# A linear-attention kernel's first step: two levels of products formed over both half chunks at once

## The chip, the cores and the metric

The kernel runs on one core of a Trainium2 chip. The metric is the device time of one execution in microseconds, as the median of several. A core has TensorE (PE in the profile, with its weight loads as PEld), VectorE (DVE), ScalarE (ACT), GpSimd (POOL) and SyncE (SP, which issues most DMAs). Each takes the instructions of its own queue in order; semaphores tie the queues together.

## The reference

Two blocks follow one another, all in fp32. The first is a linear attention with a state that decays (4 batches, 8 heads, 768 tokens, 48 channels a head); the second a feed-forward block (384 to 2048 to 384) with an activation, on the 3072 rows that the first one gives.

```python
def _attn_ref(r, k, v, w, u):
    B, H, S, D = r.shape
    state = np.zeros((B, H, D, D), dtype=np.float32)
    y = np.zeros_like(r)
    for t in range(S):
        kt, vt, rt, wt = (k[:, :, t], v[:, :, t], r[:, :, t], w[:, :, t])
        cur = np.einsum('bhd,bhe->bhde', u[None] * kt, vt)
        y[:, :, t] = np.einsum('bhd,bhde->bhe', rt, state + cur)
        state = wt[:, :, :, None] * state + np.einsum('bhd,bhe->bhde', kt, vt)
    return y.astype(np.float32)

def _moe_ref(x, w_in, w_out):
    h = x @ w_in
    sp = np.maximum(h, 0.0) + np.log1p(np.exp(-np.abs(h)))
    g = h * erf(sp)
    return (g @ w_out).astype(np.float32)
```

## The kernel before

The tokens are cut into chunks of 128, and each chunk into two half chunks of 64 (`HC`). A step handles one chunk of two batches; twelve steps follow one another. Within a step the attention of a half chunk on itself is built by levels, 1 to 6 (`LOG`): at level n the tokens stand in blocks of 2^n, and the right half of each block (`rights`) meets the left half. A level has three parts. `level_products` (L669 to 685) forms k by r on TensorE, for every pair of heads (`n`, 8 of them), every half chunk (`s0`) and the two heads of the pair (`e`), which lie on partitions 0 to 47 and 64 to 111: 8 x 2 x 2 = 32 products a level. Each product has the keys as its weights (its columns are key tokens) and 32 query tokens as its moving side. Result and half chunk share partitions: the first half chunk fills PSUM partitions 0 to 63, the second 64 to 127. `scale` (L357 for one of two batches of head pairs, L364 for all) multiplies k and r in place by decay totals, for the next level. `take_level` or `take_blocks` then copies what counts out of PSUM into `own`, which holds key tokens on partitions and query tokens along the row.

The first step is written apart, in `attend_first`. There the products of a level come in two batches of four head pairs (`halves`), each followed by its scaling, so that VectorE scales one batch while TensorE forms the other. Two PSUM tiles (`banks`) take turns. Between two levels `keep_busy` (L1008) issues a 128 x 128 by 384 matmul with zeros into the tile whose turn is next; it must wait until the level before has been copied out of it. Levels 2 to 4 are copied by VectorE with a mask (`take_level`, L691), level 5 (`MASKED`) by ScalarE in four copies of 16 partitions (`take_blocks`, L712), level 6 by ScalarE in two copies of 32 partitions (`take_level`, L698). At level 5 a product has 48 weight columns (64 less the 16 that meet nothing), at level 6 it has 32.

Behind level 6 the step goes on: eight transposes of k (L957), `from_own` (L725: `own` times v, one part before and one after the new state), `state_part` (L800), `through_state` (L751), a hop of some channels by matmul (L766), and then the second step, whose level 1 products (L681) stand around that hop. The second step takes in the first pieces of the feed-forward block: `hidden` (L1171) multiplies by w_in, 12 records at a time, between the levels. Meanwhile the weights come in and are converted: DMAs issued by SyncE, a scaling by ScalarE (L289, L297), a shift by VectorE (L306), an addition by GpSimd (L319). The order on each queue is the order in which the program's calls stand.

Of the kernel before, what the change touches and what calls it, by code (L numbers as in the profile page):

```python
# [21 lines left out]
HC = 64  # L22
# [21 lines left out]
LOG = 6  # L44
MASKED = 5
# [7 lines left out]
def rights(ap, half):  # L53

    names = "abcdefg"[: len(ap.shape) - 1]
    spread = " ".join(names)
    return ap.rearrange(f"{spread} (n two h) -> {spread} n two h", two=2, h=half)[
        (slice(None),) * len(names) + (slice(None), 1)
    ]
# [32 lines left out]
def kernel(  # L92
# [14 lines left out]
    nc = tc.nc  # L107
    PSUM = bass.MemoryType.PSUM

    n_steps, _, _, JP, C = rkw.shape  # L110
    NH, D = v.shape[2:]
    NP = JP // NJ
    NE = NH // JP
# [50 lines left out]
    def products(shape, n=None):  # L164

        if n is None:
            n = turns["next"]
            turns["next"] = 1 - n
        names = "abc"[: len(shape) - 1]
        return banks[n][:].rearrange(  # L170
            f"p ({' '.join(names)}) -> p {' '.join(names)}", **dict(zip(names, shape[1:]))
        )
# [164 lines left out]
    def rows(e, n=D):  # L337
        return slice(e * EP, e * EP + n)
# [314 lines left out]
    def parts_of(s):  # L653

        c, i = divmod(s, SPC)
        in_t, vt = loaded[s]
        made, tots, tot = ready[s]
        ends = tot.rearrange("p (n h) -> p n h", h=NC)
        return c, in_t, vt, made, states[i][c % 2], states[i][1 - c % 2], ends

    def by_pair(t):

        return lambda x, n: t[:, x, n]

    def first_pair(x, n):

        return turns["first"][:, n // NP, x, n % NP]

    def level_products(pp, rk, level, ns=range(NJ * NP)):  # L669

        half = 1 << (level - 1)
        m = HC - half if 1 < level <= MASKED else HC if level == 1 else half
        for n in ns:
            for s0 in range(0, C, HC):
                for e in range(NE):
                    right = rk(0, n)[rows(e), s0 : s0 + HC]
                    to = pp[s0 : s0 + m, e, n, :]
                    if level > 1:
                        right = rights(right, half)
                        to = to[:, : HC // 2].rearrange("p (b h) -> p b h", h=half)  # L680
                    nc.tensor.matmul(  # L681
                        to, lhsT=rk(1, n)[rows(e), s0 : s0 + m], rhs=right,
                        start=True,
                        stop=True,
                    )

    def take_level(own, pp, level):
        half = 1 << (level - 1)
        got = pp[:].rearrange("p e n t -> p (e n) t")
        if level <= MASKED:  # L690
            nc.vector.copy_predicated(  # L691
                rights(own[:], half),
                rights(mask_sb[:, level - 1 : level, :].to_broadcast([P, NH, HC]), half),
                got[..., : HC // 2].rearrange("p n (b h) -> p n b h", h=half),
            )
        else:
            for s0 in range(0, C, HC):
                nc.scalar.copy(own[s0 : s0 + half, :, half:], got[s0 : s0 + half, :, :half])  # L698
# [2 lines left out]

    def take_blocks(own, pp, level):

        half = 1 << (level - 1)
        got = pp[:].rearrange("p e n t -> p (e n) t")
        for s0 in range(0, C, HC):
            for b in range(HC // 2 // half):
                of = slice(s0 + 2 * b * half, s0 + (2 * b + 1) * half)  # L710
                t = (2 * b + 1) * half
                nc.scalar.copy(  # L712
                    own[of, :, t : t + half], got[of, :, b * half : (b + 1) * half]
                )

    def from_own(s, own, swap):
        vt = loaded[s][1]
# [170 lines left out]
    def attend_first(xT):  # L888


        for _ in prepare(0):
            pass
        totals = plan_totals(0)
        c, _, vt, made, S, S_next, ends = parts_of(0)
        t5 = turns["first"]
        own = att.tile([P, NH, HC], FP32, name="own")
        halves = [range(j * NP, (j + 1) * NP) for j in range(NJ)]
        batch = JP * C // 2 // NJ
        pp = products([P, NE, JP, HC])
        for half in halves:  # L900
            level_products(pp, by_pair(made), 1, half)
            stay_warm(2)
        nc.scalar.copy(first[:], mask_sb[:, 0, :])
        totals(1, part=slice(0, batch))
        for j in range(NJ):
            scale(0, 1, batch=j)
        load_second(t5[:, 1, 0, NP - 1, 1:2])

        def wait_for(t):

            nc.gpsimd.tensor_copy(out=block_sb[:, 0:1], in_=t5[:, 1, 0, NP - 1, t : t + 1])

        wait_for(1)
        totals(1, part=slice(batch, 2 * batch))
        totals(2, part=slice(0, batch // 2))
        nc.vector.tensor_mul(
            own[:], pp[:].rearrange("p e n t -> p (e n) t"),
            first[:, None, :].to_broadcast([P, NH, HC]),
        )
        behind = {3: (3,), 4: (4, 5), 5: (6,)}  # L920
        for level in range(2, LOG):
            pp = turns.pop("pp", None) or products([P, NE, JP, HC])
            for j, half in enumerate(halves):
                level_products(pp, first_pair, level, half)
                scale(0, level, batch=j)
            turns["pp"] = products([P, NE, JP, HC])
            keep_busy(turns["pp"], (DM,))
            (take_blocks if level == MASKED else take_level)(own, pp, level)
            wait_for(1 << level - 1)
            if level == 2:  # L930
                totals(2, part=slice(batch // 2, batch))
            else:
                totals(*behind[level])
            if level == 2:
                stages["b"](0, 0)
                stages["b"](0, 1)
                stages["r"](0)
                second = prepare(1)
                next(second)
                nc.sync.dma_start(out=vt[:], in_=v[0])  # L940
                stages["l"](1, own[:, 0, 2:3])
                nc.sync.dma_start(out=ws[1][:], in_=rkw[1][:, 2])
        totals = plan_totals(1)
        pp = turns.pop("pp")
        for j, half in enumerate(halves):
            level_products(pp, first_pair, LOG, half)
            scale(0, LOG, batch=j)
        take_level(own, pp, LOG)
        wait_for(HC - 1)
        next(second)  # L950

        kT = att.tile([P, NH, D], FP32, name="kT", bufs=1)
        kT_by_e = kT[:].rearrange("p (e n) d -> p e n d", e=NE)
        turned = products([P, JP, P])
        turns["next"] = 1 - turns["next"]
        for n in range(JP):
            nc.tensor.transpose(turned[:, n, :], first_pair(1, n), ident[:])  # L957
        from_own(0, own, 1)
        for half, copy in zip(halves, (nc.vector.tensor_copy, nc.scalar.copy)):
            copy(  # L960
                kT_by_e[:, :, half.start : half.stop],
                turned[:, half.start : half.stop].rearrange("p n (e d) -> p e n d", e=NE)[..., :D],
            )
        stages["h"](0)
        fence()
        stages["l"](2, seen[:, 0:1])
        load_v(1)
        stages["h"](0)
        ps = [[products([P, NE, JP, HC], 1 - e)[:, e] for e in range(NE)]]
        state_part(0, kT, ps, (0,))  # L970
        from_own(0, own, 0)
        nc.scalar.copy(middle[rows(1)], ps[0][1][rows(1), :, :D])
        nc.vector.tensor_copy(middle[rows(0)], ps[0][0][rows(0), :, :D])
        stages["o"](0)
        nc.gpsimd.tensor_mul(faded[1][:], middle[:], ends[:, :, 1:2].to_broadcast([P, JP, D]))
        through_state(0, xT)
        stages["b"](1, 0)
        stages["b"](1, 1)
        stages["r"](1)
        stages["h"](1)  # L980
        stages["h"](1)
        totals(1)
        stages["o"](1)
        totals(*range(2, LOG + 1))

        def pending():
            part = products([P, NE, JP, HC], turns["next"])[:, 0]
            state_part(0, kT, ps + [[part] * NE], (1,))
            nc.vector.tensor_add(S_next[both], faded[1][both], part[both, :, :D])
            load_third()  # L990
            stages["l"](5, S_next[:, 0, 0:1])

        turns["pending"] = pending
# [560 lines left out]
    for kk in range(KT):  # L1554
        n = D // KT
        to, of = (x.rearrange("p (e m) -> p e m", e=NE) for x in (apart[:, kk], ident[:]))
# [189 lines left out]
```

## Time and profile before

| what | value |
|---|---|
| median of three runs | 573.74 us |
| the three runs | 572.72, 574.93, 573.74 us |
| the profiled execution, its own time | 573.87 us |
| its span in the profile | 572.1 us |
| PE busy | 563.2 us (98% of the span) |
| DVE, ACT, POOL busy | 453.9, 358.2, 248.5 us |
| products of levels, L681: matmul records | 2368 in the program, 33.9 us busy |
| w_in products, L1171 | 960 records, 214.9 us busy |
| first step | about 0 to 26 us |
| granted TensorE clock in the first 30 us and after | 1.00 |

The page gives each engine's busy time and its share of the span; PE is a matmul's time from its start to a modelled end, and matmuls overlap, so that 98% does not mean that the array is full. An fp32 matmul appears as two records of MATMUL and two of LDWEIGHTS, so 32 products are 64 records of each. In a row `48*48 48x32` stands for weights of 48 rows by 48 columns and 32 tokens that move. "issue" as the cause of idle time means that the engine waited for nothing that the profile shows.

### The profile page before, as it was taken

How to read it: one execution, taken by the hardware profiler on the slowest of the kernel's cores; microseconds unless marked ns; L12 is line 12 of the kernel's file. 1: busy time of each engine (PE TensorE's matmuls, PEld its weight loads, DVE VectorE, ACT ScalarE, POOL GpSimd, SP SyncE). 2: the span in 40 equal slices, each digit the busy share in tenths (PEclk: the TensorE clock that was granted, in tenths of full speed). 3: DMA queues.
4: the chain of work that ended last, by engine and by line, in shares of the span. 5: the costliest groups of instructions: out<-in, count | busy, mean ns of one | idle time of the engine just before them, and what ended most of it. 6: DMA issues, size and time to landing. Idle time of an engine off the chain costs nothing.

```text
span 572.1 us, 16721 instructions
## 1 busy us (share of the span) xinstructions
PE 563.2 (98%) x7318; PEld 500.4 (87%) x7318; DVE 453.9 (79%) x505; ACT 358.2 (63%) x494; POOL 248.5 (43%) x268
## 2 busy tenths in 40 slices
PE   8899999999999999999999999999999999999997
PEld 5688887678998998998998998898898899989997
DVE  8684886999899998799699599599599596477730
ACT  3658877745458858747756766766675771489500
POOL 4757390732885883384285185176075000000000
PEclk9999999999999999999999999999999999999999
DMA  7596672440425315245245235235332201000000
GB/s 267 190 311 255 226 222 59 171 162 7 148 86 167 107 60 167 37 157 169 33 140 180 40 126 195 40 112 167 47 112 84 47 9 34 3 2 1 28 29 28
DMA packets 54081, 63.24 MB, mean 111 GB/s; under 512 B 35160, under 2 KB 40568, under 8 KB 52984
## 3 DMA queue, kind: packets, MB, share of 16 engines
q1 hardware_dynamic: 53480, 61.98, 34.5%
q8 instruction: 57, 0.93, 0.7%
q10 hardware_dynamic: 528, 0.20, 0.1%
q14 instruction: 16, 0.13, 0.1%
HBM read 52.39 MB, written 8.69 MB: 107 GB/s over the span
## 4 chain that ended last, share of the span: by engine, by line
PE 92%; DVE 4%; ACT 1%; issue 1%; DMA 1%; DVEq 0%; ACTq 0%
PE m L1171 35%; PE m L1293 33%; PE c L1396 6%; PE pp L681 6%; PE m L1203 4%; PE y L725 2%; PE y L751 2%; PE pp L800 2%; DVE in L364 1%; DMA in<-in_rkw 1%; PE pp L1081 1%; PE pp L1008 1%; DVE h L1136 1%; PE c L1293 0%; PE m L999 0%
## 5 line engine op out<-in xcount | busy, mean ns | idle before, releaser
L1171 PE MATMUL m<-xT,w_in_sb 128*128 128x256 f32 x960 | 214.9, 382 | 0.3 <-ACT h L1180 0.3
L1171 PEld LDWEIGHTS m<-xT,w_in_sb 128*128 128x128 f32 x960 | 179.9, 190 | 25.5 <-ACT h L1180 0.8
L364 DVE TENSOR_TENSOR in<-in,tot_sb 128x1024 f32<-128x1024 f32 (+1 forms) x55 | 77.8, 1415 | 6.5 <-PE pp L681 4.4
L1180 ACT COPY h<-m 128x512 f32<-128x512 f32 x80 | 46.2, 579 | 48.6 <-PE m L1171 48.4
L1293 PE MATMUL m<-mixed,h 128*128 128x192 f32 x320 | 56.7, 331 | 0.0
L1293 PE MATMUL m<-w_out_sb,h 128*128 128x192 f32 x320 | 56.1, 329 | 0.0
L1293 PEld LDWEIGHTS m<-mixed,h 128*128 128x128 f32 x320 | 51.8, 190 | 0.9
L1293 PEld LDWEIGHTS m<-w_out_sb,h 128*128 128x128 f32 x320 | 52.0, 190 | 0.5
L1293 PE MATMUL m<-w_out_sb,room 128*128 128x192 f32 x288 | 49.7, 326 | 0.0
L1293 PEld LDWEIGHTS m<-w_out_sb,room 128*128 128x128 f32 x288 | 47.3, 190 | 0.1
L1131 ACT ACT_TABLE_LOAD x28 | 35.9, 1283 | 10.7 <-DVE h L1136 8.5
L503 POOL TENSOR_TENSOR words<-words,own 128x384 f32<-128x384 f32 x21 | 30.1, 1434 | 22.8 <-DVE words L534 13.0
L544 POOL TENSOR_TENSOR words<-words 128x384 f32<-128x384 f32 x28 | 39.7, 1448 | 0.0
L681 PEld LDWEIGHTS pp<-in 48*48 48x48 f32 (+4 forms) x2368 | 30.1, 120 | 10.5 <-issue 5.8
L1127 ACT ACT_TABLE_LOAD x28 | 35.9, 1283 | 1.8 <-issue 1.3
L496 POOL TENSOR_TENSOR own<-rest 128x384 f32<-128x384 f32 x7 | 9.7, 1382 | 61.0 <-ACT o L1299 61.0
L681 PE MATMUL pp<-in 48*48 48x32 f32 (+4 forms) x2368 | 33.9, 206 | 0.0
L544 POOL TENSOR_TENSOR rk<-words 128x384 f32<-128x384 f32 x28 | 33.4, 1224 | 0.0
L569 DVE TENSOR_REDUCE sums<-rk 128x16 f32<-128x768 f32 (+2 forms) x31 | 31.6, 1020 | 0.0
L448 POOL TENSOR_TENSOR tot_sb<-tot_sb 128x256 f32<-128x256 f32 (+4 forms) x50 | 28.9, 578 | 3.8
L1127 ACT ACTIVATE room<-h 128x1024 f32<-128x1024 f32 x28 | 29.6, 1057 | 0.3
L319 POOL TENSOR_TENSOR w_out_sb<-w_out_sb,rest 128x768 int32<-128x768 int32 x8 | 18.3, 2292 | 21.6 <-DVE w_out_sb L311 21.6
(217 smaller groups left out, 1010.7 us busy)
## 6 DMA issues: line engine op xcount, KB each, us to landing
in<-in_rkw SPq DMA_DIRECT2D x8, 1024.0 KB, 5.5
words<-in_moe_w_in SPq DMA_DIRECT2D x16, 384.0 KB, 5.3
words<-in_moe_w_out SPq DMA_DIRECT2D x16, 384.0 KB, 5.8
words<-in_rk_rows SPq DMA_DIRECT2D x8, 768.0 KB, 5.9
w<-in_rkw SPq DMA_DIRECT2D x11, 512.0 KB, 7.4
v<-in_v SPq DMA_DIRECT2D x12, 384.0 KB, 5.6
out<-o SPq DMA_DIRECT2D x23, 192.0 KB, 3.0
in<-in_rkw SPq DMA_DIRECT2D x7, 512.0 KB, 5.8
```

Source lines behind the costliest of these rows:

```text
L364: nc.vector.tensor_mul(halves, halves, view(tots[level - 1], 0, [[1, n], [2, nb], [0, half]]))
L448: nc.gpsimd.tensor_mul(new, pair[:, :, 0], pair[:, :, 1])
L503: engine.tensor_mul(to, to, of[:, :, None, :].to_broadcast([P, NEAR // 2 // half, half, D]))
L544: engine.tensor_mul(to[:, i], r[:, half:], k[:, part * rows + i, None].to_broadcast([P, half, D]),)
L569: nc.vector.tensor_reduce(out=to, in_=of, axis=mybir.AxisListType.X, op=ALU.add)
L681: nc.tensor.matmul(to, lhsT=rk(1, n)[rows(e), s0 : s0 + m], rhs=right, start=True, stop=True,)
L1127: nc.scalar.activation(sp_room, chunks[0], AF.Softplus)
L1131: nc.scalar.activation(at, sp_room, AF.Erf)
L1171: nc.tensor.matmul(ps[:, ff, :], lhsT=w_in_sb[:, g * FG + f + ff, kk * P : (kk + 1) * P], rhs=xT[:, kk, :], start=kk == 0, stop=kk == KT - 1,)
L1180: nc.scalar.copy(h[:, f : f + FT, :], ps[:])
L1293: nc.tensor.matmul(to, lhsT=a[:, f], rhs=b[:, f], start=start and f == 0, stop=f == FG - 1, skip_group_check=True,)
L1396: nc.tensor.matmul(to[:, f], lhsT=turns["weights"][b][:, i * FT + f], rhs=turns["tokens"][a], start=a + b in STARTS and not f, stop=True, ...
```

## The change

A new function, `long_products`, forms the products of both half chunks at once: the weights are the keys of the whole chunk from its first token to the last that counts (112 at level 5, 96 at level 6), and all 64 query tokens that are right halves of the chunk's blocks move past them. A level has 8 x 2 = 16 such products instead of 32. Of each result only the blocks on the diagonal count; the products of one half chunk's keys with the other's queries are formed and left in PSUM. The levels 5 and 6 of the first step use it; every other step keeps `level_products`. `take_blocks` now reads the block's place along the whole chunk, in four copies of 16 partitions at level 5 as before, and it also takes level 6, in two copies of 32 partitions as `take_level` did.

```diff
+    def long_products(pp, rk, level, ns):
+
+        half = 1 << (level - 1)
+        m = C - half
+        for n in ns:
+            for e in range(NE):
+                nc.tensor.matmul(
+                    pp[:m, e, n, :].rearrange("p (b h) -> p b h", h=half),
+                    lhsT=rk(1, n)[rows(e), :m], rhs=rights(rk(0, n)[rows(e)], half),
+                    start=True, stop=True,
+                )
+
     def take_blocks(own, pp, level):
 
         half = 1 << (level - 1)
         got = pp[:].rearrange("p e n t -> p (e n) t")
-        for s0 in range(0, C, HC):
-            for b in range(HC // 2 // half):
-                of = slice(s0 + 2 * b * half, s0 + (2 * b + 1) * half)
-                t = (2 * b + 1) * half
-                nc.scalar.copy(
-                    own[of, :, t : t + half], got[of, :, b * half : (b + 1) * half]
-                )
+        for b in range(C // 2 // half):
+            of = slice(2 * b * half, (2 * b + 1) * half)
+            t = (2 * b + 1) * half % HC
+            nc.scalar.copy(
+                own[of, :, t : t + half], got[of, :, b * half : (b + 1) * half]
+            )
...
             for j, half in enumerate(halves):
-                level_products(pp, first_pair, level, half)
+                (long_products if level == MASKED else level_products)(pp, first_pair, level, half)
                 scale(0, level, batch=j)
...
         for j, half in enumerate(halves):
-            level_products(pp, first_pair, LOG, half)
+            long_products(pp, first_pair, LOG, half)
             scale(0, LOG, batch=j)
-        take_level(own, pp, LOG)
+        take_blocks(own, pp, LOG)
```

## The prediction

> **What bounds the kernel now.** I read the page first: engine times, the chain that ended last, the queues.
>
> ```profile
> span 572.1 us, 16721 instructions
> ...
> PE 563.2 (98%) x7318; PEld 500.4 (87%) x7318; DVE 453.9 (79%) x505; ACT 358.2 (63%) x494; POOL 248.5 (43%) x268
> ...
> q8 instruction: 57, 0.93, 0.7%
> ...
> PE 92%; DVE 4%; ACT 1%; issue 1%; DMA 1%; DVEq 0%; ACTq 0%
> ```
>
> TensorE (PE) ends almost everything, so time won or lost on its path in the first step should reach the end. The edit sits near 16 to 20 us, so the timeline of that stretch comes next (columns: start, time, engine, line, operation, tiles, count; in brackets the idle time before and what ended it).
>
> ```profile
> 15.99 0.96 PE L681 MATMUL pp<-in 48*48 48x32 f32 x64
> 16.25 0.70 DVE L691 COPY_PREDICATED own<-mask_sb,pp 128x512 f32<-128x512 int32 x1
> ...
> 16.93 1.34 DVE L357 TENSOR_TENSOR in<-in,tot_sb 128x512 f32<-128x512 f32 x2
> ...
> 17.00 0.91 PE L1008 MATMUL pp<-s,ident 128*128 128x384 f32 x2
> 17.04 1.49 ACT L712 COPY own<-pp 16x256 f32<-16x256 f32 x4 [1.24 <-PE pp L681]
> ...
> 17.84 0.93 PE L681 MATMUL pp<-in 48*32 48x32 f32 x64
> ...
> 18.43 1.31 DVE L357 TENSOR_TENSOR in<-in,tot_sb 128x512 f32<-128x512 f32 x2 [0.17 <-PE pp L681]
> ...
> 18.85 1.18 ACT L698 COPY own<-pp 32x512 f32<-32x512 f32 x2 [0.33 <-PE pp L681]
> ...
> 19.27 1.18 PE L957 MATMUL pp<-ident,in 128*128 128x128 f32 x8 [0.50 <-DVE in L357]
> ```
>
> An fp32 matmul is two records, each with a weight load, so 64 records are the 32 products of one level. At level five the scaling (16.93) waits for VectorE's own L691, not for the products: there is cover. At level six it waits for the products (0.17): none. Then the timeline of PE alone, further on:
>
> ```profile
> 21.68 0.73 PE L800 MATMUL pp<-v,kT 64*48 64x48 f32 x22 [0.23 <-ACT kT L960]
> 22.59 0.34 PE L800 MATMUL pp<-v,kT 64*48 64x48 f32 x7 [0.17 <-issue]
> ...
> 26.37 0.56 PE L681 MATMUL pp<-rk 48*64 48x64 f32 x18
> 28.17 0.46 PE L681 MATMUL pp<-rk 48*64 48x64 f32 x14 [1.24 <-issue]
> ```
>
> Twice PE stops inside a group of products, at no wait that the program has ("issue"). Counting PE's records, its few semaphore instructions included, the first stop stands before the 961st and the second before the 1217th: 256 apart. The page's 57 instruction packets carry 0.93 MB, 16,384 bytes each in the trace, and PE has 14,726 records in all: 258 for a packet. So PE was out of instructions: the packet that brings block 961 onward ran from 20.24 to 21.16 and its first instruction started at 22.59, 1.43 after; the next ran from 25.85 to 26.82, first use 28.17, 1.35 after. From start to start the two gaps are 0.38 and 1.46 where such records usually stand 0.04 apart: 0.34 and 1.42 us lost, both on the chain.
>
> **The change, part by part.** *Products.* Removed: 64 products of 48 or 32 weight columns by 32 tokens. Added: 32 of 112 or 96 by 64. The old ones lie in four parts of the array (two strips of rows, two halves of columns); single records show four starts 6 to 7 ns apart, then a step, and the period of the four is 59, 57, 55, 52, 45 and 32 ns at 64, 62, 60, 56, 48 and 32 columns: 5 ns and 0.84 ns a column, whether 64 or 32 tokens pass. Carried on, a pair (only the two strips remain) takes 99 ns at 112 and 86 ns at 96 columns. No row has this shape. Bounds: 56 ns, the period of the 64-token products of 48 columns (L725), if only tokens count; 109 ns, the step of the full-array transposes of L957 (128 by 128), if full width counts. I take the fit, because six widths lie on it. A batch is eight pairs: 0.72 us from first to last start at level five (now 0.36), 0.63 at level six (now 0.26).
>
> [...]
>
> Followed through: level five's first batch starts at 15.99, its last record at 16.71, its result reaches VectorE 0.32 later (0.21 to 0.25 for the record, 0.08 to the wait), at 17.03 instead of 16.93. The second batch runs from 16.81 to 17.51 and is scaled from 17.83 to 18.55 (now until 18.27). The matmul that keeps PE busy (L1008) now starts at 17.00, when L691 is done; it will start 0.15 after the last product, at 17.66, and level six 0.84 behind it, at 18.50 instead of 17.84. Its first batch ends its starts at 19.13 and is scaled from 19.45 (now 18.43); the second from 19.22 to 19.82, scaled from 20.13 (now 19.04). The transposes of the second half and `from_own` behind them come 1.07 later. ScalarE's copies keep number and shape, start at 20.14 instead of 18.85 and end by 21.31, just before the transposes do (21.45): hidden, by 0.14. **Products: +1.07 us.** The same walk with 56 ns gives +0.2, with 109 ns +1.65.
>
> *Instructions.* 32 products fewer are 128 records, half a block. The chip comes to fresh blocks at other places: those where the 833rd, 1089th, 1345th and 1601st records of before stand (24.06, 31.86 and 36.66 us for the last three). A packet starts 1.0 to 5.1 us after PE has reached the 56th record ahead of the block before it (the spread of the 57 packets, long when the other DMAs are busy), lasts 0.97, and serves 1.4 later. For 1089: that point lies 11 records into level six, 18.5; the DMA share falls from 0.73 to 0.25 at 20 us, so I put the start at 20.2 to 21.2 and the use at 23.6 at the latest; PE needs it at 24.06 + 1.07 - 0.34 = 24.8. **The first stop goes: -0.34.** For 1345: point at 23.8, DMA share 1.0 until 26 and a start up to 3.3 later, use by 29.5; needed at 31.86 - 0.69 = 31.2. **The second goes: -1.42.** For 1601: point at 30.8, share 1.07 to 0.9 from 30 to 34, start 3.2 later as for its neighbours (28.17 to 31.34), use at 36.4, needed at 36.0: **+0.4** (0 to 1). Further on the shortest spell from such a point to the need is 4.7 us, as now, against 3.4 that a packet needs.
>
> [...]
>
> *What the win runs into.* In the second step PE would come earlier than now. The products at 39.70 need a scaling of L364 that ends at 39.33, and PE's own queue is only 0.3 behind that; VectorE there hangs on weights that DMAs bring, which the +1.07 delays. I charge **+0.2** (0 to 1.4, all of it lost again).
>
> Sum: +1.07 - 0.34 - 1.42 + 0.4 + 0.2 = -0.1. Nothing else is added, moved or made to wait: the other four queues keep their instructions and order, DMAs included. The profiled run took 573.87 us (1.8 around its span), the median is 573.74; from both, **573.7 us**.
>
> **Rivals.** *The stops stay or come back elsewhere* (fetches later by what PE is later): 573.87 + 1.07 = 574.9. For it: packets wait up to 5.1 us in this stretch. Against: half a block moves the need by 0.6 to 2.4 us and the first request lies in the same busy spell. *Only the tokens count*: 0.2 - 1.76 + 0.4 = -1.2, 572.7. Against it: the six widths. *The wide products don't run in pairs*, the slower side: then each takes the pair's time alone, the walk gives 4.0 us, and 4.0 - 1.76 = +2.2, 576.1; with 109 ns for each it is 5.1, 577.2. For it: no row has two products across all columns at once. Against: four old products run at once, and two of those write the same partitions from different strips. Each 10 ns of the step from product pair to pair is worth 0.32 us (32 such steps), so from 0.10 us on it outweighs the stops, and from 0.2 us on it costs 0.5%. *That the change does not do what it says*: the instruction order has 16 products at 112 and 16 at 96; nothing to price.
>
> **How the numbers follow.** Forecast 0.57; stops stay 0.18 (574.9); only tokens 0.12 (572.7); no pairs 0.08 (576.1 to 577.2); others 0.05. A median of this kernel can be told from no change at about 0.5%, 2.9 us (the three runs span 2.2). So slower is most of "no pairs" with a stop kept, and others: 0.10; faster needs more than both stops together and would be something that I don't see: 0.04; the rest, 0.86, lies within. The range takes in the two middle rivals and the spread of the runs: 572.2 to 575.6.
>
> **What would show it.** Right: records of 112 columns in pairs, about 99 ns from pair to pair (96: 86); L1008 behind level five near 17.7; the scaling of level six near 19.4; no "issue" gap of PE at `from_own` or at level one of the second step, perhaps a short one near 36; the second step's first w_in products (L1171, now 28.55) near 27.9. Wrong: pairs at 56 or near 200 ns, a new gap over 1 us in the first 40 us, or a second step that starts early and ends where it ends now.

## The result, and the profile after

The changed kernel takes 576.08 us (median of 19 runs, 575.11 to 579.48) against 573.31 us before (19 runs, 572.60 to 576.38): a ratio of 1.0054, 95% interval 1.0039 to 1.0069. It is slower by 2.8 us, and outside the predicted range by 0.5. The profiled execution took 575.11 us, 1.24 more than the one before (573.87); it is the shortest of the 19, so its trace shows the least that the change costs.

The first lines of the page of the changed kernel, its chain by engine, and the group of the w_in products (busy time and mean ns of one; then the idle time before them and what ended it):

```profile
span 573.3 us, 16593 instructions
...
PE 564.9 (99%) x7254; PEld 503.0 (88%) x7254; DVE 453.9 (79%) x505; ACT 357.9 (62%) x494; POOL 245.0 (43%) x268
...
PE 83%; DVE 4%; ACT 1%; DMA 1%; issue 0%; ACTq 0%
...
L1182 PE MATMUL m<-xT,w_in_sb 128*128 128x256 f32 x960 | 214.7, 382 | 1.7 <-DMA xT<-y 1.5
```

There are 128 instructions fewer, and PE is busy for 1.7 us more. The issue gaps are gone from the chain ("issue" 0%, it was 1%). The last line holds the new cost: w_in products (L1182, which was L1171) once wait 1.5 us for a DMA that brings xT. Before, the same line had 0.3 us idle in all, and none of it for a DMA.

The first step and the start of the second, in PE's timeline of the changed kernel:

```profile
16.15 1.79 PE L710 MATMUL pp<-in 48*112 48x64 f32 x32
17.87 0.91 PE L1019 MATMUL pp<-s,ident 128*128 128x384 f32 x2
18.71 1.58 PE L710 MATMUL pp<-in 48*96 48x64 f32 x32
...
22.97 0.87 PE L811 MATMUL pp<-v,kT 64*48 64x48 f32 x29 [0.23 <-ACT kT L971]
...
27.25 0.69 PE L681 MATMUL pp<-rk 48*64 48x64 f32 x32
27.88 2.86 PE L1182 MATMUL m<-xT,w_in_sb 128*128 128x256 f32 x12
...
35.22 0.97 PE L681 MATMUL pp<-in 48*60 48x32 f32 x56
36.54 0.31 PE L681 MATMUL pp<-in 48*60 48x32 f32 x8 [0.35 <-issue]
```

The wide products are the two L710 groups. The L811 and L681 groups behind them are whole: the two stops of before have gone, and a new one of 0.35 us stands at 36.54. The w_in products begin at 27.88 instead of 28.55. At 44.5 us, and still at 59.5, PE stands within 0.01 us of where it stood before. Up to there the change costs nothing in this execution, and the whole loss comes in the next seven microseconds.

That stretch in PE's timeline, of the kernel before:

```profile
60.59 1.11 PE L681 MATMUL pp<-in 48*62 48x32 f32 x64
61.63 3.68 PE L1171 MATMUL m<-xT,w_in_sb 128*128 128x256 f32 x15
```

and of the changed kernel:

```profile
60.60 1.11 PE L681 MATMUL pp<-in 48*62 48x32 f32 x64
63.18 2.18 PE L1182 MATMUL m<-xT,w_in_sb 128*128 128x256 f32 x9 [1.47 <-DMA xT<-y]
```

The same work reaches the same place at 60.6, and then the w_in products start 1.55 us later, because xT is not there. xT holds what the second step's attention gives, channels on partitions, and the w_in products read it; six DMAs of 16 KB bring a part of it, issued between 59.1 and 60.7 by SyncE's and ScalarE's queues in both kernels. The view of the tile xT from 55 to 66 us gives their time from issue to landing, of the kernel before:

```profile
DMA to landing us min/median/max: 1.8/1.9/2.1
```

and of the changed kernel:

```profile
DMA to landing us min/median/max: 3.0/3.5/3.8
```

The DMA view of 60.4 to 62.5 us of the changed kernel (queue, kind, packets, MB, share of the 16 engines' time) says what shares the engines with them:

```profile
q10 hardware_dynamic: 95, 0.05, 10.1%
q1 hardware_dynamic: 92, 0.05, 8.8%
q8 instruction: 1, 0.02, 2.9%
```

In the kernel before, the stretch from 60.4 to 62.2 us has the two dynamic queues with 95 and 92 packets and no line for q8. In the changed kernel one instruction packet of 16,384 bytes runs from 60.90 to 61.86, 0.96 us, on one of the 16 DMA engines (2.9% of 16 engines' 2.1 us is 0.97 us of one); before, the neighbouring one ran from 58.79 to 59.85, ahead of xT's first packet at 60.36. Each transfer of 16 KB lands in sixteen parts. Fifteen of them land when they did before, to within 0.05 us; the sixteenth comes late, at 62.89 to 63.67 for the six transfers, and PE waits for all sixteen. The late parts of the six run one after another from 61.84 to 62.54, the first as the instruction packet ends, in turn from one queue and the other. The trace doesn't name the engine of a packet: that these parts stood behind the instruction packet on its engine is read from these times.

The shift of PE is 0.00 at 59.5 us, +1.55 at 61.6, +1.34 at 66 and +1.22 at 560: nothing else of size happens to it in this execution.

### The profile page after: what moved, and what is told of

Its sections match the earlier page's. It is cut to its first block, busy times and chain, and to the rows that moved or that the text cites. A ratio compares the mean times of both kernels' runs of the same rounds, so it can differ in the third digit from the quotient of the medians.

```text
span 573.3 us, 16593 instructions
## 1 busy us (share of the span) xinstructions
PE 564.9 (99%) x7254; PEld 503.0 (88%) x7254; DVE 453.9 (79%) x505; ACT 357.9 (62%) x494; POOL 245.0 (43%) x268
## 2 busy tenths in 40 slices
DMA packets 54081, 63.24 MB, mean 110 GB/s; under 512 B 35160, under 2 KB 40568, under 8 KB 52984
## 4 chain that ended last, share of the span: by engine, by line
PE 83%; DVE 4%; ACT 1%; DMA 1%; issue 0%; ACTq 0%
PE m L1304 33%; PE m L1182 31%; PE c L1407 6%; PE m L1214 4%; PE pp L681 4%; PE y L736 2%; PE y L762 2%; PE pp L811 1%; DVE in L364 1%; DMA xT<-y 1%; DVE h L1147 1%; PE pp L1092 1%; PE c L1304 0%; DVE sums L569 0%; PE pp L824 0%
## 5 line engine op out<-in xcount | busy, mean ns | idle before, releaser
L1182 PE MATMUL m<-xT,w_in_sb 128*128 128x256 f32 x960 | 214.7, 382 | 1.7 <-DMA xT<-y 1.5
L1182 PEld LDWEIGHTS m<-xT,w_in_sb 128*128 128x128 f32 x960 | 180.4, 190 | 26.3 <-ACT rest L297 1.6
L364 DVE TENSOR_TENSOR in<-in,tot_sb 128x1024 f32<-128x1024 f32 (+1 forms) x55 | 78.0, 1418 | 7.6 <-PE pp L681 6.8
L681 PEld LDWEIGHTS pp<-in 48*48 48x48 f32 (+4 forms) x2240 | 28.8, 120 | 9.7 <-issue 4.2
L681 PE MATMUL pp<-in 48*48 48x32 f32 (+4 forms) x2240 | 32.4, 207 | 0.3 <-issue 0.3
L319 POOL TENSOR_TENSOR w_out_sb<-w_out_sb,rest 128x768 int32<-128x768 int32 x8 | 17.1, 2140 | 22.7 <-DVE w_out_sb L311 22.6
```

The costliest lines, as they stand in the source:

```text
L364: nc.vector.tensor_mul(halves, halves, view(tots[level - 1], 0, [[1, n], [2, nb], [0, half]]))
L681: nc.tensor.matmul(to, lhsT=rk(1, n)[rows(e), s0 : s0 + m], rhs=right, start=True, stop=True,)
L1182: nc.tensor.matmul(ps[:, ff, :], lhsT=w_in_sb[:, g * FG + f + ff, kk * P : (kk + 1) * P], rhs=xT[:, kk, :], start=kk == 0, stop=kk == KT - 1,)
```

## The experiments

The theory tested first and last (A): the change costs what it does because it takes 128 records, half a block of 256, out of PE's stream (the stops of before stand at the 961st and the 1217th record; counted alike, the stop at 36.54 of the changed kernel stands at the 1473rd, 256 further on). All later blocks then begin at other work, and one of their packets meets the transfer of xT. Its rivals are that the time goes into the wide products and what they delay, wherever the blocks lie, or that instruction stops of PE come back. To tell them apart, blocks are moved by small matmuls that nobody reads, 4 records each, and the products are changed without the blocks.

### Small matmuls in the first step

```diff
+    def pad(count):
+
+        spare = products([P, NE, JP, HC], turns["next"])
+        for i in range(count):
+            e, s0 = i % NE, i // NE % NC * HC
+            nc.tensor.matmul(
+                spare[s0 : s0 + NEAR, e, 0, :NEAR], lhsT=ident[rows(e), :NEAR],
+                rhs=ident[rows(e), :NEAR], start=True, stop=True,
+            )
...
+        pad(32)
         turned = products([P, JP, P])
```

In `attend_first`, ahead of the transposes, in the changed kernel: 128 records put the later blocks back where they were before, by the count of records.

> The changed kernel with 32 small matmuls of the identity (16 columns by 16 tokens, results overwritten) ahead of the first step's transposes: 128 PE records more, so that every instruction block from there on begins where it begins in the kernel before. Theory A (the blocks' place decides: an instruction packet meets the transfer of xT in the second step): the 1.5 us wait of the w_in products for xT goes, the packet near 58.8 is there again, time 573.3 to 574.6 with the wide products' own cost of about 1.1 us and the early stops back. Theory B (the wide products themselves cost it): 576.0 or more, as the changed kernel or worse by up to 0.4 us for the 32 matmuls.

574.82 us (573.83 to 576.79), ratio to before 1.0027 [1.0014, 1.0040]. It does the work of the changed kernel and 32 matmuls more, and is 1.3 us faster (576.08 to 574.82). Its instruction packet runs from 60.15 to 61.39, xT's first at 61.49, and xT lands in 2.2 us (median). It stays 1.5 above before. In its profile PE is only 0.10 behind before at 36.7: neither early stop is there, although the blocks lie as before again, and that pays for the wide products and the pads. Then PE waits 0.92 us at 44.6 for a scaling by VectorE (L364), and 0.3 is lost at xT.

The same 32 in the kernel before, whose blocks then lie as the changed kernel's:

> The kernel before with the same 32 small matmuls: the products of levels 5 and 6 are the old ones, but the instruction blocks begin half a block away from before, as in the changed kernel (128 records more instead of 128 fewer, of 256). Theory A: about the changed kernel's time, 575 to 577, with PE waiting about 1.5 us for xT near 61.6 and an instruction packet near 60.9. Theory B: 573.3 to 573.9, no such wait.

579.68 us (577.72 to 582.10), ratio 1.0119 [1.0092, 1.0146]. Slower, but more than the theory's share: a stop of PE stands early in its timeline,

```profile
20.18 0.33 PE L968 MATMUL pp<-ident,in 128*128 128x128 f32 x1
22.86 0.93 PE L968 MATMUL pp<-ident,in 128*128 128x128 f32 x7 [2.35 <-issue]
```

and in its windows (busy time and instructions of PE, weight loads, DVE, ACT and POOL, then the granted clock, DMA share and GB/s) half the clock behind it:

```profile
24.00:26.00 2.00, 1.88 (x54) 1.55 (x46) 1.46 (x4) 0.48 (x1) 0.58 (x2) 0.52 0.03 8
26.00:28.00 2.00, 2.00 (x76) 2.00 (x76) 0.55 (x1) 0.47 (x1) 2.00 (x2) 0.50 0.84 255
```

The spell at half clock lasts 6.83 us. I read it as the pads using up instructions faster than they are brought; a packet of that stretch was not moved by itself. Before xT it is already 3.94 us behind; at xT its packet (64.21 to 65.16) does meet the transfer, and it loses 0.8 more. As a test of the theory alone this run is spoilt by its own pads.

Half as many pads, a quarter of a block, in the changed kernel:

> The changed kernel with 16 such matmuls: blocks a quarter away from both. Theory A: the packet that follows 2600 records or so is asked for some 0.5 to 3 us earlier than in the changed kernel and passes before or after the transfer of xT; time between 573 and 575 unless another transfer is met. Theory B: 576.

576.64 us (573.97 to 581.41), ratio 1.0065 [1.0038, 1.0092]. In its profile packet (63.05 to 64.01) and transfer (from 63.41) meet, and PE's shift grows from 3.07 to 5.43 us there, in two waits for xT (0.56 and 1.49). The 3.07 is older: PE stops for instructions at 36.5 (1.04) and at 50.6 (1.78).

And in the kernel before:

> The kernel before with 16 such matmuls: blocks a quarter away on the other side. Theory A: a time of its own, by which transfers the packets meet; anything from 572.5 to 577 and different from before. Theory B: 573.3 to 573.7, as before.

577.84 us (576.25 to 581.77), ratio 1.0086 [1.0059, 1.0114]. Its packet (63.74 to 65.19) meets only the last pieces of xT, which land in up to 3.7 us where the median is 2.1; the shift goes from 2.01 to 3.83. The 2.01 is a wait of PE for ScalarE (L428) at 46.3.

### Half the products left out

In the kernel before, with the blocks moved but less work and no wide product: the second half chunk's products of levels 5 and 6 are left out.

```diff
-    def level_products(pp, rk, level, ns=range(NJ * NP)):
+    def level_products(pp, rk, level, ns=range(NJ * NP), upto=C):
...
-            for s0 in range(0, C, HC):
+            for s0 in range(0, upto, HC):
...
-                level_products(pp, first_pair, level, half)
+                level_products(pp, first_pair, level, half, HC if level == MASKED else C)
...
-            level_products(pp, first_pair, LOG, half)
+            level_products(pp, first_pair, LOG, half, HC)
```

> The kernel before, with the second half chunk's products of levels 5 and 6 left out in the first step (those results are not formed): 128 PE records fewer, as in the changed kernel, and no wide product. The remaining products keep their period, so levels 5 and 6 take what they took. Theory A (instruction blocks half a block away: the early stops go, but the packet near 60.9 meets the transfer of xT): first w_in products near 26.8 to 27.5, a PE wait for xT of 1 to 2 us near 61.5, time 573.0 to 575.5, so not faster although work is left out. Theory B (the wide products cost it): the stops gone and nothing lost, 571.5 to 572.5.

574.74 us (573.65 to 578.33), ratio 1.0018 [0.9998, 1.0038]. With 32 products less than before, none of them wide, it is not faster. Its profiled execution was its longest, and shows what happens at xT (PE's timeline):

```profile
60.75 1.11 PE L681 MATMUL pp<-in 48*62 48x32 f32 x64
62.78 1.32 PE L1171 MATMUL m<-xT,w_in_sb 128*128 128x256 f32 x4 [0.92 <-DMA xT<-y]
65.56 2.27 PE L1171 MATMUL m<-xT,w_in_sb 128*128 128x256 f32 x5 [1.47 <-DMA xT<-y]
```

Two waits for xT, with the kernel's old products and an instruction packet from 60.37 to 61.46; from 65.77 the granted clock is 0.50 for 3.41 us. The wide products are not needed for the loss. The changed kernel, with as many PE instructions and 576.01 us on the same chip, is 1.3 above this run: that is 32 wide products against 32 old ones, and whatever else differs by then.

### The same pads ahead of the transfer and behind it

The cleanest pair leaves the first step of the changed kernel alone. In `attend`, 32 pads behind `from_own` of the second step, so that the blocks are back at their old work before xT moves:

```diff
         from_own(s, own, 1)
+        if s == 1:
+            pad(32)
         ps = products([P, JP, P])
```

> The changed kernel with the 32 small matmuls (16 columns by 16 tokens, 0.45 us) in the second step ahead of its transposes, near 51 us: up to there as the changed kernel, behind it the instruction blocks stand as in the kernel before. Theory A: the packet near 60.9 moves back to about 58.8, no PE wait for xT, time 573.3 to 574.3. Theory B: 576.5, the changed kernel plus the small matmuls.

and the same with `if s == 2`, in the third step, when xT has long landed:

> The same small matmuls in the third step, near 90 us, behind the transfer of xT. Theory A with the loss in the second step alone: 576.0 to 576.6, the wait for xT as in the changed kernel. If transfers of later steps are met too: between 574.5 and 575.8. Theory B: 576.5.

with the changed kernel itself once more, on the same chip:

> The changed kernel unchanged, for a second profile and the spread of its runs beside these: 575.1 to 579.5, median 576.1. Theory A: PE waits for xT in the second step again, by another amount; if the profiled run is slower than 575.1 the longer wait shows where.

| kernel | median, us | range, us | ratio to before |
|---|---|---|---|
| pads in the second step | 574.71 | 573.57 to 575.97 | 1.0012 [0.9996, 1.0029] |
| pads in the third step | 576.50 | 574.91 to 580.07 | 1.0048 [1.0029, 1.0068] |
| changed kernel again | 576.01 | 575.12 to 580.16 | 1.0048 [1.0029, 1.0068] |

Same wide products, same number of instructions in the first two rows: 1.8 us apart by the place of the pads alone. With the pads ahead of the transfer the kernel cannot be told from before, though PE is 0.65 us behind before at 52 us, 0.62 of it through them. In the third step they cost the same 0.62 (PE's shift around 81 us). PE's timeline with the pads in the second step,

```profile
61.36 1.11 PE L681 MATMUL pp<-in 48*62 48x32 f32 x64
62.40 4.30 PE L1194 MATMUL m<-xT,w_in_sb 128*128 128x256 f32 x17
```

and in the third:

```profile
59.73 1.11 PE L681 MATMUL pp<-in 48*62 48x32 f32 x64
62.35 3.91 PE L1194 MATMUL m<-xT,w_in_sb 128*128 128x256 f32 x17 [1.51 <-DMA xT<-y]
```

Without the wait the products follow 1.04 us behind the start of the level's, with it 2.62. The xT landings are 2.2 and 3.7 us (medians).

The repeat of the changed kernel was profiled in an execution of 578.91 us, and shows what the longer runs hold. ScalarE's timeline has the issues of xT by its queue (ACTq),

```profile
60.28 3.07 ACTq L797 DMA_DIRECT2D xT<-y  x2
```

PE's timeline the products that need it,

```profile
61.07 1.11 PE L681 MATMUL pp<-in 48*62 48x32 f32 x64
63.39 1.30 PE L1182 MATMUL m<-xT,w_in_sb 128*128 128x256 f32 x4 [1.21 <-DMA xT<-y]
66.29 3.90 PE L1182 MATMUL m<-xT,w_in_sb 128*128 128x256 f32 x10 [1.59 <-DMA xT<-y]
```

and the windows behind it, columns as above:

```profile
64.00:66.00 2.00, 0.69 (x3) 0.29 (x2) 1.68 (x2) 1.53 (x3) 0.00 (x0) 0.98 0.92 334
66.00:68.00 2.00, 1.71 (x4) 1.47 (x5) 2.00 (x3) 1.72 (x2) 1.62 (x1) 0.50 0.84 286
68.00:70.00 2.00, 2.00 (x7) 1.60 (x7) 1.97 (x3) 0.20 (x1) 1.06 (x1) 0.66 0.91 348
```

The loss has three stages here. The packet comes a little earlier against the transfer (60.68 to 62.07; xT from 60.84), and now ScalarE's own queue is held: its two last issues of xT take 3.07 us, where they take 1.46 in the changed kernel's first profile, and the last starts at 62.5 instead of 60.7. It lands 3.6 later, at 66.15, and there ends PE's second wait. PE has by then done 1.3 us of work in some four, and from 65.93 the granted clock is 0.50 for 3.41 us. All in all PE's shift grows from 0.48 to 5.09 us.

The run's mean clock of 0.997 fits: 3.41 us at half clock are 1.7 of 573. Of the 31 runs of the changed kernel six have a mean clock of 0.994 to 0.997, and they take 577.98 to 580.16 us; the other 25 show 0.999 or 1.000 and take 575.11 to 578.20. With the pads in the second step all 12 runs show 1.000. The kernel before has such runs too (0.997 at 574.6 to 576.4 us); what lies behind those was not profiled.

### Other places

The kernel before with 32 pads in the second step, to bring the loss about with no other change:

> The kernel before with the 32 small matmuls in the second step, near 51 us: the first step and all of the second up to there as before; behind it the instruction blocks stand half a block away. They cost 0.65 us by the profile of the changed kernel with them. Theory A: the packet comes near 61 and PE waits for xT: 575.5 to 577.5, with no wide product in it, and some runs with a spell at half clock. Theory B (the loss belongs to the first step): 573.3 + 0.65 = 574.0.

577.64 us (576.57 to 581.74), ratio 1.0084 [1.0058, 1.0110]. The packet (61.92 to 63.24) meets the transfer (from 61.95), xT lands in 3.3 us, and the shift grows from 1.60 to 2.73 us there. In the 1.60 is a stop of 2.0 us at the pads, of their own making, so only a part of the 4 us is the transfer. The first 50 us of this kernel are the same as before, and its PE timeline says something of the old stops:

```profile
22.26 0.87 PE L800 MATMUL pp<-v,kT 64*48 64x48 f32 x29 [0.23 <-ACT kT L970]
...
26.55 0.69 PE L681 MATMUL pp<-rk 48*64 48x64 f32 x32
```

Neither group is broken: the packets ran at 18.93 and 23.30, not at 20.24 and 25.85. The two stops that the change was to save do not happen in every execution of the same instructions.

The changed kernel with 16 and with 48 pads in the second step:

> The changed kernel with 16 small matmuls in the second step (about 0.35 us): the block is asked for 64 records sooner than in the changed kernel. Theory A: the packet starts near 59.5 to 60.3 instead of 60.9 and overlaps the transfer of xT (60.4 to 62.3 here) less; the wait is 0 to 1.5 us; 574.0 to 575.8. Theory B: 576.4.

575.53 us (573.67 to 578.78), ratio 1.0044 [1.0027, 1.0060]. Packet from 60.69 to 61.65, transfer from 60.63: they meet, and the shift grows by 0.74, and by 80 us to 1.41 in all.

> The changed kernel with 48 small matmuls in the second step (about 0.95 us): the blocks then stand a quarter ahead of before. Theory A: one packet is through before 59 us and the next is asked for only with the level 2 products near 61.5, so it starts near 62.5 or later, behind the transfer of xT: no wait, 574.3 to 575.3 despite the most padding. Theory B: 577.0.

577.77 us (577.32 to 579.20), ratio 1.0081 [1.0065, 1.0096]. Here the packet (64.21 to 65.17) met only the last piece of xT, with a PE wait of 1.43 us. A stop for instructions of 1.07 us stands at 37.7, ahead of the pads: it is the short stop of the changed kernel (0.35 at 36.54 in its first profile), longer in this execution. Where a packet falls could not be placed to the microsecond by counting records: it also hangs on how far PE is and, as I read it, on how busy the DMAs are (in the profile of before the packet at 58.79 starts 1.0 us after its point, as the prediction counts it, with no other packet between; the one at 43.44 starts 3.5 us after, with the DMA share at 1.01). Theory A's ranges held for three of the ten kernels with pads or without half the products (pads in the third step, 16 in the second, half the products); three medians lie 0.1 to 0.4 us above them, and four lie 0.8 to 2.7 above (32 and 16 pads in the first step of before, 16 in the first and 48 in the second step of the changed kernel). It says where the loss comes, and does not give its size.

The profiles side by side, times in us; the shift is how far PE stands behind the kernel before, at the same work around 59.5 and 66:

| kernel | packet | xT's first packet | xT landing, median/max | shift |
|---|---|---|---|---|
| before | 58.79–59.85 | 60.36 | 1.9/2.1 | |
| changed | 60.90–61.86 | 60.36 | 3.5/3.8 | 0.00 to 1.34 |
| changed again | 60.68–62.07 | 60.84 | 3.6/3.7 | 0.48 to 5.09 |
| changed, 32 first step | 60.15–61.39 | 61.49 | 2.2/2.2 | 1.13 to 1.43 |
| before, 32 first step | 64.21–65.16 | 64.29 | 3.1/3.2 | 3.94 to 4.76 |
| changed, 16 first step | 63.05–64.01 | 63.41 | 3.0/3.5 | 3.07 to 5.43 |
| before, 16 first step | 63.74–65.19 | 62.36 | 2.1/3.7 | 2.01 to 3.83 |
| before, half the products | 60.37–61.46 | 60.51 | 3.4/3.5 | 0.15 to 4.55 |
| changed, 32 second step | 60.01–60.94 | 61.00 | 2.2/2.3 | 0.77 to 0.96 |
| changed, 32 third step | 59.45–60.83 | 59.48 | 3.7/3.8 | -0.86 to 0.51 |
| before, 32 second step | 61.92–63.24 | 61.95 | 3.3/3.6 | 1.60 to 2.73 |
| changed, 16 second step | 60.69–61.65 | 60.63 | 3.1/3.3 | 0.40 to 1.14 |
| changed, 48 second step | 64.21–65.17 | 62.51 | 2.6/3.4 | 2.14 to 3.64 |

In the two moved kernels whose packet is over when xT begins, as it is before, 0.2 and 0.3 us are lost there; in the ten profiles where they meet, 0.7 to 4.6. In these ten PE waits thirteen times, and each time it goes on 0.13 to 0.14 us after the last part of a transfer of xT has landed; that holds too for "before, 32 second step" and "changed, 16 second step", where the profile names ScalarE's L291 as what ended the wait (1.26 and 0.87 us). Four of them lose another 0.5 to 0.7 us between 70 and 80 us, which the table leaves out. No version here is faster than the kernel before.

## Why the prediction was wrong

By its own steps:

- *Products, +1.07: right.* Sixteen pairs of 112 columns stand 98 to 99 ns apart (99 forecast), those of 96 columns 85 ns (86). L1019 behind level five starts at 17.87 (17.66 forecast; this execution began its level five 0.16 later than before). The scaling of level six starts at 19.71 against 18.43; less those 0.16 it is +1.12. The rival without pairs named 576.1 and slower, which is what came, but its mechanism did not: the records stand in pairs.
- *Instructions near the edit: right in the profiled execution.* Both stops went, and the short one near 36 came (gap of 0.56 at 36.0; 0.4 forecast). In other executions of these instructions it is absent (the repeat) or 1.07 (48 pads in the second step).
- *The two stops as a gain, -1.76: mis-sized for the median.* The term was read from one execution; the kernel before with pads in the second step runs the same instructions without either stop, and the changed kernel with 32 pads in the first step has neither with its blocks in the old place. How often before has them was not counted.
- *What the win runs into, +0.2: right in the profiled execution.* Shift -0.15 at 36.7 us and 0.00 at 44.5, against -0.1 for the sum. With 32 pads in the first step the same stretch costs 1.0.
- *Two readings that did not decide it.* The period of four products does not stay the same "whether 64 or 32 tokens pass": at 48 columns it is 45 ns with 32 tokens (L681) and 56 with 64 (L751, L725); at 112 and 96 columns the fit held all the same. And by the prediction's own count the packet at 31.34 starts 6.8 us after its point (24.57), so 5.1 is not the longest.
- *The step that failed* is the one that closed the account of the packets: "Further on the shortest spell from such a point to the need is 4.7 us, as now, against 3.4 that a packet needs", and with it "Nothing else is added, moved or made to wait: the other four queues keep their instructions and order, DMAs included". The first asks too little: behind 36.54 PE does not stop for instructions again in the changed kernel's profile, as it says. The second is wrong in "made to wait": the DMAs of xT keep their order and wait. It put the cost of a moved packet to the DMAs at nothing. I looked at each moved packet only as something that PE waits for. It is also a transfer of 0.96 us on a DMA engine, and what it holds up was not looked at. The packet near 60 us was in time for PE, and it held up xT: +1.55 us in the mildest run.

For the median, 2.8 us above before (2.5 on the chip of the repeat, 576.01 against 573.51), the profile accounts for 1.24, all of it lost at xT. Moving the blocks back ahead of xT takes 1.3 us off the changed kernel's median on that chip (576.01 to 574.71), although the pads cost some 0.6; so about 1.9 of the 2.5 comes from the place of the packet. This is an estimate from those numbers. What is left, some 0.6, is of the size of a wide-product cost that the stops repay only in some runs; that is argued and not shown. Nor is it shown how often a run has the second wait without the fall of the clock: runs of the changed kernel between 576 and 578 us were not profiled (with 16 pads in the first step one run has it).

## What to carry to other kernels

Here 128 PE records fewer moved the instruction packets behind them: one ran from 60.90 us, where the neighbouring one of before ran from 58.79, and one part in sixteen of each xT transfer came late (median landing 3.5 us, 1.9 before). When an edit adds or removes instructions on the engine that bounds the kernel, list the packets behind it as transfers, with start and end, and look which small, urgent DMAs they will meet; asking whether the engine itself starves is half the question. And a gain that is a stop in one profiled execution should be seen in a second one before it is booked.

## What the runs showed of the hardware

- One instruction packet of 16,384 bytes ran for 0.96 us (60.90 to 61.86, changed kernel). The six DMAs of 16 KB that it met land in sixteen parts: fifteen came as before, one late, and the time from issue to landing was 3.5 us, against 1.9 before (medians).
- Two waits of 2.8 us together, with 1.3 us of work between them, were followed by 3.41 us at a granted clock of 0.50 in the repeat of the changed kernel. PE was not idle throughout the stretch before the fall. With half the products left out, waits of 0.92 and 1.47 us were followed by the same spell; with 16 pads in the first step, waits of 0.56 and 1.49 us were not.
- fp32 products of 48 rows and 32 tokens step in fours, at 5 ns and 0.84 ns a weight column (45 ns at 48 columns, 57 at 62). The wide ones, with 64 tokens, lie on the same line in pairs: 85 ns at 96 columns, 98 to 99 at 112. Tokens are not free everywhere: at 48 columns 64 of them make it 56 ns (L751).
- PE stood still 0.17 to 2.35 us at "issue" in these runs, inside groups of short matmuls. In the changed kernel the packet ahead of its stop ended at 35.12, and PE went on at 36.54.
